# Sparse attention with a feed-forward block: sampled, end and neighbouring keys gathered into one buffer, and edge queries without their zero half

## The chip, the cores and the metric

The kernel runs on 1 core of one Trainium2 chip. The metric is the device time of one execution in microseconds (us). The kernel before takes 754.68 us as the median of 3 runs (754.65 to 762.38). The change is judged by the same metric on the same kind of chip.

## The reference

```python
batch, n_heads, seq, head_dim = (4, 8, 768, 64)     # q, k, v: float32
block, n_rand = 32, 3                               # 24 blocks of 32 positions
scores = scale * np.matmul(q, k.transpose(0, 1, 3, 2))
mask = np.abs(blk_i - blk_j) <= 1                   # neighbouring blocks
mask = mask | (blk_i == 0) | (blk_j == 0) | (blk_i == n_blocks - 1) | (blk_j == n_blocks - 1)
for qb in range(n_blocks):
    for kb in sampled_blocks[qb]:                   # 3 sampled blocks for each block of queries
        mask[qb * block:(qb + 1) * block, kb * block:(kb + 1) * block] = True
scores = np.where(mask, scores, -1000000000.0)
attn = np.exp(scores - np.max(scores, axis=-1, keepdims=True))
attn = attn / (np.sum(attn, axis=-1, keepdims=True) + 1e-09)
x = np.matmul(attn, v)                              # then (tokens, 512)
h = x @ w_in                                        # 512 -> 2048
g = h * erf(np.maximum(h, 0.0) + np.log1p(np.exp(-np.abs(h))))
return g @ w_out                                    # 2048 -> 512
```

A query of one of the 22 middle blocks sees 8 blocks of keys: the first and the last block of the sequence, three neighbours (its own and one on each side) and three sampled ones. A query of the first or the last block (an edge query) sees all 24.

## The kernel before, in words

The attention of one batch is cut into **units**. A middle unit `("m", b, u)` is two neighbouring middle blocks of queries in all 8 heads; there are 11 in a batch and 44 in all. An edge unit `("f", b, pr)` is the first and the last block of queries for one pair of heads; there are 4 in a batch and 16 in all. The feed-forward work is cut into groups of 256 tokens by 256 hidden values (`ff_first`, `ff_logs` and what follows); there are 96.

`scores` (lines 624 to 648) makes a unit's scores on TensorE in float32. `kx` holds one batch's keys in SBUF: two heads of 64 values one above the other on the 128 partitions (`a` is 0 or 1, the upper or the lower head of a pair), 24 blocks, 4 pairs of heads, 32 positions. For a middle unit it issues 32 small products, each of 64 rows by 32 queries. The 16 of `part` 0 take 96 columns (the three neighbours) from `kx`. The 16 of `part` 1 take 160 columns from `kbufs`: the first block, three sampled ones and the last one. There is one buffer for each block of queries, 4 in all. The scores of head half `a` lie in columns 512 `a` to 512 `a` + 511 of a PSUM tile of 128 partitions by 1024 columns; pair `pr` writes partitions 32 `pr` to 32 `pr` + 31.

For an edge unit `order_q` has copied the queries into `qm`, which is zero elsewhere, so that one product over all 128 rows gives both heads of a pair: the queries of `a` = 0 stand in the upper half of the rows, those of `a` = 1 in the lower half, and the zeros keep the heads apart. That is two products of 128 by 128, with 512 and 256 columns.

`gather` (lines 331 to 354) fills the key buffers on GpSimd (POOL): six copies of one sampled block (128 columns) a unit, and the two end blocks (256 columns) once a buffer and batch. `gather_v` (lines 359 to 386) brings the same blocks of values by DMA: neighbours and ends by SP, the sampled rows by an indirect DMA of POOL. Their order within a buffer has to be that of the score columns.

The first six units and the preparation of the weights come first, in an order that a scheduler chooses. From then on (`held`) each engine has its instructions in the order in which the loop over groups (lines 987 to 1042) emits them. One round of the loop issues on TensorE: the products with the values of an earlier unit (`po`), `ff_first` of one group (`h`, 24 products), the scores of one unit, `ff_second` of an earlier group (`o`, 12 products). Some rounds have no unit. `gathers` runs before `scores` in a round, so the keys of the next unit are asked for one round ahead; POOL's copies then wait until the unit that last read the buffer has its scores.

All instructions that these helpers record carry line 48 in the profile, so groups are told apart by the names of their tiles: `s_m` and `s_f` are the scores of middle and edge units, `kbuf` and `kx` the keys, `h` and `o` the feed-forward products.

Of the kernel before, what the change touches and what calls it, by code (L numbers as in the profile page):

```python
# [9 lines left out]
F32 = mybir.dt.float32  # L10
I32 = mybir.dt.int32
# [7 lines left out]
P = 128  # L19
BLOCK = 32  # L20
# [11 lines left out]
def sparse_attention_moe(ctx: ExitStack, tc: tile.TileContext, qT, kT, v, sampled, w_in, w_out, out):  # L32
# [26 lines left out]
    B, H, D, S = qT.shape  # L59
    NB = S // BLOCK  # L60
# [5 lines left out]
    NR = sampled.shape[1]  # L66
    KT = S // P
    HP = H // 2
# [74 lines left out]


    qts = {}
    qm = cp.tile([P, HP, 2, 2, BLOCK], F32, tag="qm", name="qm")
    dve.memset(qm, 0.0)

    def load_q(b, t):
        if b == 0 and 0 < t < 4:  # L150
# [12 lines left out]
    def queries(b, u):  # L163
        t, half = divmod(u, 2)
        return qts[b, t][:, :, half * 2 * BLOCK : (half + 1) * 2 * BLOCK].rearrange("p r (j c) -> p r j c", c=BLOCK)

    def order_q(b):
        qt = queries(b, NU)
        for a in range(2):
            dve.tensor_copy(qm[a * D : (a + 1) * D, :, :, a, :], qt[a * D : (a + 1) * D])  # L170

    QW = 4 * VW
    vraws = {}
# [20 lines left out]
    def pow2_bound(bound, tag, by_sum):  # L194

        top = st.tile([P, 1], F32, tag="top", name=f"top_{tag}")
        dve.reduce_max(top, bound, AX.X)
        if by_sum:  # L200
            allm = ps_h.tile([P, W], F32, tag="h", name=f"allm_{tag}")
            if tag[0] == "v":
                pe.matmul(allm[0:1, 1 : 1 + P], top, eye, start=True, stop=True)
                top = st.tile([P, 1], F32, tag="top", name=f"most_{tag}")[0:1]
                dve.reduce_max(top, allm[0:1, 1 : 1 + P], AX.X)
            allm = allm[:, :1]
            pe.matmul(allm, ones[: top.shape[0]], top, start=True, stop=True)
        else:
            allm = st.tile([P, 1], F32, tag="allm", name=f"allm_{tag}")
            pool.partition_all_reduce(allm, top, P, bass.bass_isa.ReduceOp.max)  # L210
        return allm

    def pow2_scale(allm, tag, squared):
        m = st.tile([P, 1], F32, tag="m", name=f"m_{tag}")
        dve.tensor_scalar_max(m, allm, 1e-37 if squared else 1e-19)
        e = st.tile([P, 1], I32, tag="e", name=f"e_{tag}")
        dve.tensor_scalar(e, m.bitcast(I32), 24 if squared else 23, None, ALU.logical_shift_right)
        zero = 63 if squared else 127
        s = st.tile([P, 1], F32, tag="s_" + tag[:2], name=f"s_{tag}", bufs=2)
        inv = st.tile([P, 1], F32, tag="i_" + tag[:2], name=f"i_{tag}", bufs=2)  # L220
        unit = float(1 << 23)
        dve.tensor_scalar(s.bitcast(I32), e, -unit, (127 + 13 + zero) * unit, ALU.mult, ALU.add)
        dve.tensor_scalar(inv.bitcast(I32), e, unit, (127 - 13 - zero) * unit, ALU.mult, ALU.add)
        return s, inv
# [101 lines left out]
    rows_of = []  # L326
    vgs = {}
    kgs, last_of = {}, {}
    kbufs = [cp.tile([P, NR + 2, HP, BLOCK], F32, tag=f"kg{n}", name=f"kbuf{n}") for n in range(KGS)]

    def gather(b, u):

        first, last = 1 + 2 * u, 3 + 2 * u
        (load,), blocks = nc.values_load_multi_w_load_instructions(
            samp[0:1, first * NR : last * NR],
            [mybir.EngineType.Pool],
            min_val=0,
            max_val=NB - 1,
            skip_runtime_bounds_check_because="sampled blocks are numbers of the sequence's blocks",
        )  # L340
        tc.keep_in_program_order(load)
        for i in range(first, last):
            n = (b * NM + i - 1) % KGS
            kg = kbufs[n]
            if last_of.get(n) != b:
                last_of[n] = b
                pool.tensor_copy(kg[:, 0 : NR + 2 : NR + 1], kxs[b][:, 0 : NB : NB - 1])
            for r in range(NR):
                n = blocks[(i - first) * NR + r]
                pool.tensor_copy(  # L350
                    kg[:, 1 + r].rearrange("p a c -> p (a c)"),
                    kxs[b].rearrange("p n a c -> p n (a c)")[:, bass.ds(n, 1), :].rearrange("p n c -> p (n c)"),
                )
            kgs[b, i] = kg

    ends_of = {}
    turn_of = [0]
# [1 line left out]
    def gather_v(b, i):  # L359

        n = turn_of[0] % VGS
        turn_of[0] += 1
        vg = vbufs[n]
        tab = vtab[b]
        if i < 0:
            rows = tab[: NB * BLOCK].rearrange("(k p) c -> p k c", p=P)
            sp.dma_start(vg, rows[:, -2 * i - 2 : -2 * i])
            ends_of.pop(n, None)
        else:
            low, high = max(i - 1, 1), min(i + 2, NB - 1)  # L370
            c = (low - i + 1) * BLOCK
            sp.dma_start(vg[c : c + (high - low) * BLOCK, 0], tab[low * BLOCK : high * BLOCK])
            if high - low < 3:
                c = 0 if i == 1 else 2 * BLOCK
                sp.dma_start(vg[c : c + BLOCK, 0], tab[NB * BLOCK :])
            if ends_of.get(n) != b:
                ends_of[n] = b
                ends = tab[: NB * BLOCK].rearrange("(n r) c -> r n c", r=BLOCK)[:, 0 : NB : NB - 1]
                sp.dma_start(vg[NR * BLOCK :], ends)
            pool.indirect_dma_start(  # L380
                out=vg[: NR * BLOCK, 1],
                out_offset=None,
                in_=tab,
                in_offset=bass.IndirectOffsetOnAxis(ap=rows_of[0][: NR * BLOCK, i - 1 : i], axis=0),
            )
        vgs[b, i] = vg
# [237 lines left out]
    def scores(unit):  # L624
        kind, b, n = unit
        s = ps_s.tile([P, 1024], F32, tag="s", name=f"s_{kind}_{b}_{n}")
        kx = kxs[b]
        if kind == "m":
            qt = queries(b, n)
            s5 = s.rearrange("p (a j c) -> p a j c", a=2, j=2)  # L630
            for part in range(2):
                for j in range(2):
                    i = 1 + 2 * n + j
                    for pr in range(HP):
                        for a in range(2):
                            o, d = slice(pr * BLOCK, (pr + 1) * BLOCK), slice(a * D, (a + 1) * D)
                            if part == 0:
                                place, keys = s5[o, a, j, : 3 * BLOCK], kx[d, i - 1 : i + 2, pr, :]
                            else:
                                place, keys = s5[o, a, j, 3 * BLOCK :], kgs[b, i][d, :, pr, :]  # L640
                            pe.matmul(place, qt[d, pr, j], keys, start=True, stop=True)
            softs[unit] = (s, HP, 256)
        else:
            q_ = qm[:, n].rearrange("p n a c -> p (n a c)")
            for c, e in ((0, 512), (512, S)):
                keys = kx[:, c // BLOCK : e // BLOCK, n, :]
                pe.matmul(s[:, c:e], q_, keys, start=True, stop=True)
            softs[unit] = (s[:, :S], 1, S)

    xTs = {}  # L650
# [3 lines left out]
    def values(b, u, part):  # L654
        po = ps_po.tile([P, 512], F32, tag="po", name=f"po_{b}_{u}_{part}")
        groups = range(4) if part is None else range(2 * part, 2 * part + 2)
        for gr in groups:
# [7 lines left out]
            for x, part_of, off in terms:  # L665
                for k in range(2 if u < NU else KT):
                    for a in range(2):
                        pr = 2 * p2_ + a
                        c = (2 * pr + r) * VW
                        w = slice(c + part_of.start, c + part_of.stop)  # L670
                        for j in range(2):
                            if u < NU:
                                pT = pts["m", b, u][:, (2 * r + j) * 4 + x * 2 + k]
                                vg = vgs[b, 1 + 2 * u + j][:, k, w]
                                col = pr * BLOCK
                            else:
                                pT = pts["f", b, pr][:, x * KT + k]
                                vg = vgs[b, -1 - k // 2][:, k % 2, w]
                                col = j * 64 + r * BLOCK
                            todo.append((2 * a + j, pT[:, col : col + BLOCK], vg, at_gr + off))  # L680
            for m, (o, lhs, rhs, c) in enumerate(todo):
                pe.matmul(
# [8 lines left out]
    def norm(b, u, part):  # L691
# [1 line left out]
        tag = f"{b}_{u}_{part}"  # L693
        gr = slice(0, 4) if part is None else slice(2 * part, 2 * part + 2)
        n = gr.stop - gr.start
        rinv = st.tile([P, 4], F32, tag="rinv", name=f"rinv_{tag}")[:, :n]
        first = 0 if part is None else 1
        dve.tensor_scalar(rinv, po[:, first * PO + D : (first + n - 1) * PO + D + 1 : PO], EPS * 2.0**P_SHIFT, None, ALU.add)
        dve.reciprocal(rinv, rinv)
# [145 lines left out]
    def next_queries(m):  # L845

        b, n = divmod(m, per)
        if n == NU - 1:
            order_q(b)
# [231 lines left out]
```

## Time and profile before

| what | value |
|---|---|
| median of 3 runs | 754.68 us (754.65 to 762.38) |
| the profiled execution's own time | 764.91 us |
| its span | 763.1 us |
| granted TensorE clock, mean | 0.975 |
| TensorE (PE) busy | 686.3 us, 90% |
| ScalarE (ACT) busy | 591.9 us, 78% |
| VectorE (DVE) busy | 575.4 us, 75% |
| GpSimd (POOL) busy | 201.6 us, 26% |

The durations further down come from the one profiled execution, whose span begins with its first instruction and ends with its last. PE counts matmuls; PEld counts weight loads, which overlap them. A float32 product has two matmul records and two weight loads in the trace (16 products of a unit are 32 records), and records of small products that run side by side overlap, so that a group's busy time is less than its count times its mean.

### The profile page before, as it was taken

How to read it: one execution, taken by the hardware profiler on the slowest of the kernel's cores; microseconds unless marked ns; L12 is line 12 of the kernel's file. 1: busy time of each engine (PE TensorE's matmuls, PEld its weight loads, DVE VectorE, ACT ScalarE, POOL GpSimd, SP SyncE). 2: the span in 40 equal slices, each digit the busy share in tenths (PEclk: the TensorE clock that was granted, in tenths of full speed). 3: DMA queues.
4: the chain of work that ended last, by engine and by line, in shares of the span. 5: the costliest groups of instructions: out<-in, count | busy, mean ns of one | idle time of the engine just before them, and what ended most of it. 6: DMA issues, size and time to landing. Idle time of an engine off the chain costs nothing.

```text
span 763.1 us, 24883 instructions
## 1 busy us (share of the span) xinstructions
PE 686.3 (90%) x10400; PEld 450.6 (59%) x10400; DVE 575.4 (75%) x1122; ACT 591.9 (78%) x1023; POOL 201.6 (26%) x413
## 2 busy tenths in 40 slices
PE   1336887998999999999999999999999999999997
PEld 0213554655655666666566666666666666667663
DVE  6983999978777788778687878787777786665453
ACT  2544999878877887878888887888788887776774
POOL 3026624303364313130533312033433120000000
PEclk9976998998999999999999999999999999999999
DMA  8999835896599999855997799938988677130000
GB/s 304 415 293 283 257 91 119 195 224 154 136 224 211 193 208 182 212 144 87 250 191 162 187 166 194 251 89 185 223 157 182 130 147 168 29 77 2 8 29 27
DMA packets 188048, 129.36 MB, mean 170 GB/s; under 512 B 137760, under 2 KB 160928, under 8 KB 186912
## 3 DMA queue, kind: packets, MB, share of 16 engines
q1 hardware_dynamic: 173584, 84.50, 54.1%
q10 hardware_dynamic: 8464, 25.43, 10.4%
q0 software_dynamic: 5888, 17.84, 9.6%
q8 instruction: 81, 1.33, 0.7%
q14 instruction: 31, 0.25, 0.1%
HBM read 82.81 MB, written 12.95 MB: 125 GB/s over the span
## 4 chain that ended last, share of the span: by engine, by line
PE 78%; DMA 6%; DVE 5%; ACT 5%; issue 3%; SPq 2%; ACTq 0%; DVEq 0%
PE h L48 31%; PE o L48 31%; PE s_m L48 7%; PE po_None L48 4%; PE s_f L48 3%; SPq L48 2%; DMA vbuf<-vtab 2%; DMA wo<-in_w_in_dram 2%; DMA vtab<-vn 1%; ACT x L48 1%; PE po L48 1%; DVE room L48 1%; DMA vbuf<-in_v_dram 1%; ACT pf_m L48 1%; DVE less_m L48 1%
## 5 line engine op out<-in xcount | busy, mean ns | idle before, releaser
L48 PE MATMUL h<-xT,wi 128*128 128x256 f16 x2304 | 272.3, 275 | 5.0 <-DVE y L48 4.5
L48 PE MATMUL o<-wo,g 128*128 128x512 f16 x1152 | 264.5, 379 | 0.5 <-DVE g L48 0.2
L48 PEld LDWEIGHTS <-wi 128*128 128x128 f16 x2304 | 223.7, 99 | 45.8 <-DVE y L48 4.6
L48 ACT ACTIVATE x<-x 128x512 f32<-128x512 f32 x288 | 181.6, 631 | 8.9
L48 PEld LDWEIGHTS <-g 128*128 128x128 f16 x1152 | 109.5, 98 | 127.4 <-issue 6.6
L48 POOL DMA_INDIRECT vbuf<-vtab,idx x88 | 96.5, 1097 | 185.1 <-PE po_None L48 130.3
L48 DVE SCALAR_TENSOR_TENSOR y<-y,x 128x512 f32<-128x512 f32 x96 | 67.1, 699 | 95.0 <-ACT x L48 91.6
L48 POOL COPY kbuf<-kx 128x128 f32 (+1 forms) x280 | 87.3, 357 | 94.4 <-PE s_m L48 79.8
L48 ACT ACTIVATE x<-h,isg 128x512 f32<-128x512 f32 x96 | 65.4, 682 | 49.2 <-PE h L48 31.9
L48 ACT ACTIVATE y<-y 128x512 f32<-128x512 f32 x96 | 59.7, 622 | 32.9 <-DVE y L48 32.9
L48 ACT ACTIVATE pf_m<-s_m,less_m 128x256 f32<-128x256 f32 x176 | 68.9, 473 | 19.7 <-DVE less_m L48 18.7
L48 DVE SCALAR_TENSOR_TENSOR g<-y,sums,g 128x512 f16<-128x512 f32 x96 | 73.1, 762 | 3.4
L48 DVE SCALAR_TENSOR_TENSOR y<-y,h 128x512 f32<-128x512 f32 x96 | 65.2, 679 | 0.1
L48 ACT ACTIVATE y<-x 128x512 f32<-128x512 f32 x96 | 60.4, 631 | 3.0
L48 DVE TENSOR_REDUCE less_m<-s_m 128x4 f32<-128x1024 f32 x44 | 53.6, 1218 | 11.7 <-PE s_m L48 11.6
L48 PEld LDWEIGHTS <-pT_m 128*32 128x32 f16 x3168 | 35.4, 98 | 33.9 <-issue 31.4
L48 PE MATMUL po_None<-vbuf,pT_m 128*32 128x65 f16 (+2 forms) x3168 | 41.9, 205 | 13.2 <-issue 12.5
L48 PE MATMUL s_m<-kbuf,qt 64*32 64x160 f32 x1408 | 48.2, 316 | 3.7 <-issue 2.8
L48 DVE TENSOR_SCALAR g<-y,sums 128x512 f16<-128x512 f32 x96 | 48.0, 500 | 3.4
L48 PE MATMUL s_m<-kx,qt 64*32 64x96 f32 x1408 | 31.6, 259 | 20.4 <-ACT kx L48 13.3
L48 DVE SCALAR_TENSOR_TENSOR p_m<-pf_m,p_m 128x1024 f16<-128x1024 f32 x38 | 46.4, 1221 | 0.3 <-issue 0.3
L48 DVE TENSOR_TENSOR x<-xf,x 128x256 f16<-128x256 f32 x44 | 18.8, 426 | 31.7 <-ACT x L48 31.6
(110 smaller groups left out, 609.8 us busy)
## 6 DMA issues: line engine op xcount, KB each, us to landing
vbuf<-vtab SPq DMA_DIRECT2D x80, 195.0 KB
vraw<-in_v_dram ACTq DMA_DIRECT2D x9, 768.0 KB
vtab<-vn SPq DMA_DIRECT2D x16, 390.0 KB
vbuf<-vtab SPq DMA_DIRECT2D x12, 520.0 KB
wo<-in_w_out_dram ACTq DMA_DIRECT2D x6, 1024.0 KB
qt<-in_qT_dram SPq DMA_DIRECT2D x20, 256.0 KB
kr<-in_kT_dram ACTq DMA_DIRECT2D x12, 384.0 KB
vbuf<-vtab SPq DMA_DIRECT2D x32, 130.0 KB
```

The source lines that it names most:

```text
L48: done = call(*args, **kwargs)
```

## The change

`gather` now fills one buffer of 14 blocks for a unit instead of two of 5. Its slots are: first, three sampled, last (of the first block of queries); four neighbouring blocks `first - 1` to `last`; first, three sampled, last (of the second block of queries). The four neighbours are one new POOL copy of 512 columns. The first block of queries reads slots 0 to 7, the second slots 6 to 13, both 8 blocks, so `scores` issues 16 products of 256 columns where it issued 32, and reads `kx` no more. For the second block of queries the neighbours now come ahead of ends and samples, so `gather_v` places its values in that order. An edge unit issues four products of 64 rows by 64 queries (two heads, two pieces of columns) straight from the loaded queries; `qm` and `order_q` are gone. Several small statistics tiles have fewer buffers.

```diff
@@ load and order queries
-    qm = cp.tile([P, HP, 2, 2, BLOCK], F32, tag="qm", name="qm")
-    dve.memset(qm, 0.0)
...
-    def order_q(b):
-        qt = queries(b, NU)
-        for a in range(2):
-            dve.tensor_copy(qm[a * D : (a + 1) * D, :, :, a, :], qt[a * D : (a + 1) * D])
...
-        top = st.tile([P, 1], F32, tag="top", name=f"top_{tag}")
+        top = st.tile([P, 1], F32, tag="top", name=f"top_{tag}", bufs=1)
...
-    kbufs = [cp.tile([P, NR + 2, HP, BLOCK], F32, tag=f"kg{n}", name=f"kbuf{n}") for n in range(KGS)]
+    kbufs = [cp.tile([P, 14, HP, BLOCK], F32, tag=f"kg{n}", name=f"kbuf{n}") for n in range(KGS // 2)]
...
-        for i in range(first, last):
-            n = (b * NM + i - 1) % KGS
-            kg = kbufs[n]
-            if last_of.get(n) != b:
-                last_of[n] = b
-                pool.tensor_copy(kg[:, 0 : NR + 2 : NR + 1], kxs[b][:, 0 : NB : NB - 1])
+        n = (b * NU + u) % (KGS // 2)
+        kg = kbufs[n]
+        if last_of.get(n) != b:
+            last_of[n] = b
+            for j in range(2):
+                pool.tensor_copy(kg[:, 9 * j : 9 * j + 5 : 4], kxs[b][:, 0 : NB : NB - 1])
+        pool.tensor_copy(kg[:, 5:9], kxs[b][:, first - 1 : last + 1])
+        for j in range(2):
             for r in range(NR):
-                n = blocks[(i - first) * NR + r]
+                n = blocks[j * NR + r]
                 pool.tensor_copy(
-                    kg[:, 1 + r].rearrange("p a c -> p (a c)"),
+                    kg[:, 9 * j + 1 + r].rearrange("p a c -> p (a c)"),
                     kxs[b].rearrange("p n a c -> p n (a c)")[:, bass.ds(n, 1), :].rearrange("p n c -> p (n c)"),
                 )
-            kgs[b, i] = kg
+        kgs[b, u] = kg
...
-            for part in range(2):
-                for j in range(2):
-                    i = 1 + 2 * n + j
-                    for pr in range(HP):
-                        for a in range(2):
-                            o, d = slice(pr * BLOCK, (pr + 1) * BLOCK), slice(a * D, (a + 1) * D)
-                            if part == 0:
-                                place, keys = s5[o, a, j, : 3 * BLOCK], kx[d, i - 1 : i + 2, pr, :]
-                            else:
-                                place, keys = s5[o, a, j, 3 * BLOCK :], kgs[b, i][d, :, pr, :]
-                            pe.matmul(place, qt[d, pr, j], keys, start=True, stop=True)
+            for j in range(2):
+                for pr in range(HP):
+                    for a in range(2):
+                        o, d = slice(pr * BLOCK, (pr + 1) * BLOCK), slice(a * D, (a + 1) * D)
+                        keys = kgs[b, n][d, 6 * j : 6 * j + 8, pr, :]
+                        pe.matmul(s5[o, a, j], qt[d, pr, j], keys, start=True, stop=True)
             softs[unit] = (s, HP, 256)
         else:
-            q_ = qm[:, n].rearrange("p n a c -> p (n a c)")
+            qt = queries(b, NU).rearrange("p r j c -> p r (j c)")
             for c, e in ((0, 512), (512, S)):
-                keys = kx[:, c // BLOCK : e // BLOCK, n, :]
-                pe.matmul(s[:, c:e], q_, keys, start=True, stop=True)
+                for a in range(2):
+                    d = slice(a * D, (a + 1) * D)
+                    keys = kx[d, c // BLOCK : e // BLOCK, n, :]
+                    pe.matmul(s[d, c:e], qt[d, n], keys, start=True, stop=True)
```

The order of the instructions shows it at three places. On TensorE, unit 5 of batch 2, between the feed-forward products `h` and `o` (in brackets stand the engines whose semaphores an instruction waits for). Before:

```order
L48 MATMUL h_1_2_1_7331<-xT_1_2_5590,wi_123 128x256
L48 MATMUL s_m_2_5_7386<-kx_2_5383,qt_2_2_6797 32x96 [waits DVE_49,Activation_49]
L48 MATMUL s_m_2_5_7386<-kx_2_5383,qt_2_2_6797 32x96 x15
L48 MATMUL s_m_2_5_7386<-kbuf2_121,qt_2_2_6797 32x160 [waits Pool_49]
L48 MATMUL s_m_2_5_7386<-kbuf2_121,qt_2_2_6797 32x160 x7
L48 MATMUL s_m_2_5_7386<-kbuf3_122,qt_2_2_6797 32x160 [waits Pool_49]
L48 MATMUL s_m_2_5_7386<-kbuf3_122,qt_2_2_6797 32x160 x7
L48 LDWEIGHTS g_1_1_6_7230
L48 MATMUL o_1_2_6404<-wo_124,g_1_1_6_7230 128x512
```

The same unit in the changed kernel:

```order
L48 MATMUL h_1_2_1_6935<-xT_1_2_5262,wi_119 128x256
L48 MATMUL s_m_2_5_6991<-kbuf1_118,qt_2_2_6431 32x256 [waits DVE_49,Activation_49,Pool_49]
L48 MATMUL s_m_2_5_6991<-kbuf1_118,qt_2_2_6431 32x256 x7
L48 MATMUL s_m_2_5_6991<-kbuf1_118,qt_2_2_6431 32x256 [waits Pool_49]
L48 MATMUL s_m_2_5_6991<-kbuf1_118,qt_2_2_6431 32x256 x7
L48 LDWEIGHTS g_1_1_6_6834
L48 MATMUL o_1_2_6068<-wo_120,g_1_1_6_6834 128x512
```

Three places at which TensorE waits have become two, and the first of them now waits for POOL as well.

On TensorE, the first edge unit of batch 2 in the changed kernel; before, there stood one product of 128 by 512 and one of 128 by 256 from `qm`:

```order
L48 MATMUL s_f_2_0_8342<-kx_2_5053,qt_2_5_7733 64x512 [waits DMAHW5_49,PE_49,Activation_49]
L48 MATMUL s_f_2_0_8342<-kx_2_5053,qt_2_5_7733 64x512
L48 MATMUL s_f_2_0_8342<-kx_2_5053,qt_2_5_7733 64x256 x2
L48 LDWEIGHTS g_2_0_0_8215 [waits DVE_49]
L48 MATMUL o_2_0_8347<-wo_120,g_2_0_0_8215 128x512 [waits Activation_49]
```

Two products have become four, which alternate between the upper and the lower head.

On POOL, the copies of one middle unit in the changed kernel (`ISA` rows set the address of a sampled block); before, there were the same six copies of 128x128, into two buffers:

```order
L327 TENSOR_LOAD samp_103
L48 COPY kbuf1_118<-kx_1_2151 128x512
L48 ISA
L48 COPY kbuf1_118<-kx_1_2151 128x128
L48 ISA
L48 COPY kbuf1_118<-kx_1_2151 128x128
...
L48 DMA vbuf3_107<-vtab_1_112,idx_242 96x1040
L48 DMA vbuf4_108<-vtab_1_112,idx_242 96x1040
```

One copy of 512 columns comes ahead of the six, and the two indirect DMAs of the values stand behind all seven.

## Rows read from the trace of the kernel before

**Rows 1.** The page, its first line and section 1.
```profile
span 763.1 us, 24883 instructions
...
PE 686.3 (90%) x10400; PEld 450.6 (59%) x10400; DVE 575.4 (75%) x1122; ACT 591.9 (78%) x1023; POOL 201.6 (26%) x413
```

**Rows 2.** The page, section 4: the chain of waits, shares by engine.
```profile
PE 78%; DMA 6%; DVE 5%; ACT 5%; issue 3%; SPq 2%; ACTq 0%; DVEq 0%
```

**Rows 3.** Busy time by stretch: bounds, length, engines (instructions), TensorE clock, DMA share, GB/s.
```profile
100.00:128.00 28.00, 22.07 (x262) 16.02 (x261) 27.57 (x69) 27.61 (x53) 7.58 (x10) 0.89 0.36 91
...
400.00:500.00 100.00, 99.51 (x1584) 66.21 (x1586) 80.30 (x154) 84.20 (x146) 24.75 (x48) 1.00 0.98 191
```

**Rows 4.** Groups of PE by shape: count | busy us, mean ns | idle before, releasers.
```profile
L48 PE MATMUL s_f<-kx,qm 128*128 128x512 f32 x32 | 16.5, 597 | 0.1
...
L48 PE MATMUL s_f<-kx,qm 128*128 128x256 f32 x32 | 9.5, 379 | 0.0
```

**Rows 5.** Timeline of PE, one middle unit: start, length, operation, count.
```profile
361.53 0.56 PE L48 MATMUL s_m<-kx,qt 64*32 64x96 f32 x32
361.88 0.86 PE L48 MATMUL s_m<-kbuf,qt 64*32 64x160 f32 x32
362.67 2.76 PE L48 MATMUL o<-wo,g 128*128 128x512 f16 x12
```

**Rows 6.** Busy time of instructions on s_m by stretch; PE is the first number.
```profile
240.00:296.00 56.00, 7.45 (x320) 4.90 (x320) 6.08 (x5) 8.09 (x21) 1.00 0.98 194
...
380.00:456.00 76.00, 9.58 (x448) 6.62 (x448) 8.51 (x7) 12.27 (x32) 1.00 0.94 178
...
128.00:640.00 512.00, 55.19 (x2304) 35.31 (x2304) 43.85 (x36) 56.08 (x144) 0.99 0.88 181
```

**Rows 7.** Timeline of PE, a middle unit with pauses inside it.
```profile
297.37 0.56 PE L48 MATMUL s_m<-kx,qt 64*32 64x96 f32 x32
297.73 0.65 PE L48 MATMUL s_m<-kbuf,qt 64*32 64x160 f32 x15
298.89 0.47 PE L48 MATMUL s_m<-kbuf,qt 64*32 64x160 f32 x3 [0.52 <-issue]
299.63 0.56 PE L48 MATMUL s_m<-kbuf,qt 64*32 64x160 f32 x14 [0.27 <-issue]
300.13 2.76 PE L48 MATMUL o<-wo,g 128*128 128x512 f16 x12
```

**Rows 8.** Timeline of PE, one edge unit.
```profile
472.30 1.46 PE L48 MATMUL s_f<-kx,qm 128*128 128x512 f32 x4
473.59 1.67 PE L48 MATMUL o<-wo,g 128*128 128x512 f16 x7
```

**Rows 9.** The chain of waits in order of time: start, length, what.
```profile
358.87 2.73 PE h L48 x24
361.60 1.14 PE s_m L48 x62
362.74 2.69 PE o L48 x12
...
463.71 2.62 PE h L48 x24
466.33 2.59 PE o L48 x12
```

**Rows 10.** Groups of POOL by shape.
```profile
L48 POOL COPY kbuf<-kx 128x128 f32 x264 | 80.2, 346 | 80.4 <-PE s_m L48 79.8 <-POOL kbuf L48 0.2
L48 POOL COPY kx<-kr 128x768 f32<-128x768 f32 x12 | 10.3, 856 | 52.0 <-DMA kr<-in_kT_dram 52.0
L48 POOL COPY kbuf<-kx 128x256 f32<-128x256 f32 x16 | 8.5, 533 | 14.0 <-ACT kx L48 11.9 <-POOL kx L48 2.0
```

**Rows 11.** Timeline of POOL between two middle units.
```profile
362.60 1.48 POOL L48 COPY kbuf<-kx 128x128 f32 x6 [7.82 <-PE s_m L48]
```

**Rows 12.** Groups of DVE by shape: the copies into qm.
```profile
L48 DVE COPY qm<-qt 64x256 f32<-64x256 f32 x8 | 2.8, 352 | 0.1
```

More of the change, by code (lines that the diff above doesn't have):

```diff
@@ L203, in pow2_bound @@
                 pe.matmul(allm[0:1, 1 : 1 + P], top, eye, start=True, stop=True)
-                top = st.tile([P, 1], F32, tag="top", name=f"most_{tag}")[0:1]
+                top = st.tile([P, 1], F32, tag="top", name=f"most_{tag}", bufs=1)[0:1]
                 dve.reduce_max(top, allm[0:1, 1 : 1 + P], AX.X)
@@ L208, in pow2_bound @@
         else:
-            allm = st.tile([P, 1], F32, tag="allm", name=f"allm_{tag}")
+            allm = st.tile([P, 1], F32, tag="allm", name=f"allm_{tag}", bufs=1)
             pool.partition_all_reduce(allm, top, P, bass.bass_isa.ReduceOp.max)
@@ L213, in pow2_scale @@
     def pow2_scale(allm, tag, squared):
-        m = st.tile([P, 1], F32, tag="m", name=f"m_{tag}")
+        m = st.tile([P, 1], F32, tag="m", name=f"m_{tag}", bufs=1)
         dve.tensor_scalar_max(m, allm, 1e-37 if squared else 1e-19)
-        e = st.tile([P, 1], I32, tag="e", name=f"e_{tag}")
+        e = st.tile([P, 1], I32, tag="e", name=f"e_{tag}", bufs=1)
         dve.tensor_scalar(e, m.bitcast(I32), 24 if squared else 23, None, ALU.logical_shift_right)
         zero = 63 if squared else 127
-        s = st.tile([P, 1], F32, tag="s_" + tag[:2], name=f"s_{tag}", bufs=2)
-        inv = st.tile([P, 1], F32, tag="i_" + tag[:2], name=f"i_{tag}", bufs=2)
+        s = st.tile([P, 1], F32, tag="s_" + tag[:2], name=f"s_{tag}", bufs=1)
+        inv = st.tile([P, 1], F32, tag="i_" + tag[:2], name=f"i_{tag}", bufs=1)
         unit = float(1 << 23)
@@ L370, in gather_v @@
             low, high = max(i - 1, 1), min(i + 2, NB - 1)
-            c = (low - i + 1) * BLOCK
-            sp.dma_start(vg[c : c + (high - low) * BLOCK, 0], tab[low * BLOCK : high * BLOCK])
+            odd = i % 2
+            near, end = odd * BLOCK, 0 if odd else NR * BLOCK
+            c = near + (low - i + 1) * BLOCK
+            sp.dma_start(vg[c : c + (high - low) * BLOCK, odd], tab[low * BLOCK : high * BLOCK])
             if high - low < 3:
-                c = 0 if i == 1 else 2 * BLOCK
-                sp.dma_start(vg[c : c + BLOCK, 0], tab[NB * BLOCK :])
+                c = near + (0 if i == 1 else 2 * BLOCK)
+                sp.dma_start(vg[c : c + BLOCK, odd], tab[NB * BLOCK :])
             if ends_of.get(n) != b:
@@ L378, in gather_v @@
                 ends = tab[: NB * BLOCK].rearrange("(n r) c -> r n c", r=BLOCK)[:, 0 : NB : NB - 1]
-                sp.dma_start(vg[NR * BLOCK :], ends)
+                sp.dma_start(vg[end : end + BLOCK], ends)
             pool.indirect_dma_start(
-                out=vg[: NR * BLOCK, 1],
+                out=vg[near : near + NR * BLOCK, 1 - odd],
                 out_offset=None,
@@ L678, in values @@
                                 vg = vgs[b, -1 - k // 2][:, k % 2, w]
-                                col = j * 64 + r * BLOCK
+                                col = r * 64 + j * BLOCK
                             todo.append((2 * a + j, pT[:, col : col + BLOCK], vg, at_gr + off))
@@ L695, in norm @@
         n = gr.stop - gr.start
-        rinv = st.tile([P, 4], F32, tag="rinv", name=f"rinv_{tag}")[:, :n]
+        rinv = st.tile([P, 4], F32, tag="rinv", name=f"rinv_{tag}", bufs=2)[:, :n]
         first = 0 if part is None else 1
@@ L847, in next_queries @@
         b, n = divmod(m, per)
-        if n == NU - 1:
-            order_q(b)
         if n < NU - 1 and n % 2 == 0 and (b or n >= 6):
```

## The prediction

> **What bounds the kernel now.** I read the first section of the page, then the chain of waits, then the busy time by stretch. TensorE is busy 90% of the span and no other engine over 78% [rows 1]; 78% of the chain that ended last is TensorE's [rows 2]. In the stretch from 400 to 500 us TensorE is busy 99.5 of 100 us at full clock, while ScalarE has 84 and VectorE 80 [rows 3]. So from about 128 us on, once the preparation is over, a microsecond taken off TensorE comes off the end, and one added there is paid in full. Before that VectorE and ScalarE are busy 27.6 of 28 us [rows 3], so TensorE's scores are cheap there. The timeline of TensorE shows the place of the change: a middle unit's scores stand between `h` and `o` with no pause on either side [rows 5].
>
> **Middle units, before.** A float32 record takes 597 ns with 512 columns and 379 with 256 [rows 4]; the difference, 218 ns for 256 columns, is 0.85 ns a column. An edge unit agrees: four records, twice 512 and twice 256 columns, 1536 x 0.85 = 1.31 us, and from its first start to the next product it takes 473.59 - 472.30 = 1.29 [rows 8]. In a middle unit 32 records of 96 columns pass in 361.88 - 361.53 = 0.35 us [rows 5]. One of them needs 82 ns, so 32 x 82 / 350 = 7.5 are under way at once: all eight places that products of 64 rows by 32 queries have in the array. Per unit the streaming is then 4 x (96 + 160) x 0.85 = 0.87 us. This unit takes 1.14 us in the chain [rows 9], so 0.27 us are not streaming: 0.02 in the first part (0.35 - 4 x 0.082) and the rest in the second (0.79 - 4 x 0.136 = 0.25). It is among the shortest. Five units between 240 and 296 us and seven between 380 and 456 us (64 records each) are busy 7.45 + 9.58 = 17.03 us, 1.42 each [rows 6]; the last records overlap the next product by 0.56 + 0.86 - 0.21 - 1.14 = 0.07 us (the two parts, less their own overlap, against the 1.14) [rows 5], so they hold TensorE for 1.35.
>
> **Middle units, after.** The columns are the same, so the 0.87 us stay. What goes is half of the records and one of three waits, that between the neighbours' and the other keys' products (the order of the instructions shows them). The cost of one piece of 256 columns has no row. Its lower bound is 0.89 us, streaming with the overhead of the first part alone; the upper one is the present 1.35, if the irregular time comes from what stands around the scores and not from their split. I take 1.08, a little under the 1.14 of the shortest unit, as that unit still has the second part's start. The gain is 0.27 us a unit. Between 128 and 640 us there are 36 units (2304 records) [rows 6]: 9.7 us. The other 8 lie in the preparation, where I count nothing.
>
> **Edge units.** Two products of 128 rows become four of 64 rows by 64 queries, for the upper and lower head, on opposite quarters of the array. If the two heads run side by side, the streaming stays at 1.29 us [rows 8]. New is that the array changes from one shape of product to another on the way in and out. The nearest rows: `o` takes 2.69 us in the chain behind a middle unit's scores and 2.59 behind `h`, and `h` 2.73 where another shape stands ahead of it and 2.62 behind `o` [rows 9], 0.1 us a change. Twice that for 16 units is 3.2 us more. Bounds: nothing, and the full second pass told of below.
>
> **POOL.** 44 copies of 512 columns are added. The nearest rows are 533 ns for 256 columns and 856 for 768 [rows 10]; between them lies about 0.7, and the slope from 128 to 256 columns (346 to 533) would give 0.91. At 0.9 that is 40 us on an engine with 201.6 busy [rows 1]. It lies beside TensorE's work: the six copies wait 79.8 us for `s_m` [rows 10], that is, they start as soon as the scores that last read the buffer are done, and one set takes 1.48 us from 362.60 [rows 11], and the scores that need it come two rounds later, each of at least 2.62 + 1.14 + 2.59 = 6.35 us [rows 9]: over 12 us on. The products' first wait is now for POOL too, and all of `o` stands behind it on TensorE; with 10 us of room left it is met early. The indirect DMAs behind the copies start up to 0.9 us later; their values are used three rounds on. If that cover were gone, 36 x 0.9 = 32 us would stand on the path.
>
> **The rest.** VectorE loses 8 copies of 352 ns [rows 12] and a memset, which lie beside TensorE's work: nothing. The queries' tile is now read until the last edge unit and refilled one unit later, so SP's load finds it free: nothing. Fewer buffers of the statistics: nothing, as writer and reader follow each other anyway. In the preparation the scheduler has put VectorE's and ScalarE's work in another order, and the first scores need one more copy (0.9 us) before VectorE wants them: no estimate better than nothing, with 3 us either way.
>
> **Sum.** -9.7 + 3.2 = -6.5 us. The profiled execution took 764.9 us (its span is 763.1), so 758.4 of its kind; it is 10.2 us over the median. Against the median of 754.7 the same difference gives **748.2 us**. Bounds of the terms: -16.6 (0.89 a unit, no price for the edge units) to +3.2, each 3 us wider for the preparation: 735 to 761.
>
> **Rivals.**
> *One head waits for the other in edge units* (slower). In middle units the two heads write different halves of the score tile, columns 0 to 511 and 512 to 1023. In edge units both write the same columns, on different partitions, from different rows of the array. No row of before has two such products at once. If they take turns, an edge unit streams 1.29 us more: 16 x 1.29 = 20.6, and 748.2 + 20.6 = 768.8. It decides from 6.5 / 16 = 0.4 us a unit on. Against it: the four pairs of heads of a middle unit also write the same columns on different partitions and do run at once, though from the same rows. [...]
>
> *Records start in strict order* (no change). Each product is two records on the same place of the array. If the second held up the next product, an edge unit's records of 0.43, 0.43, 0.43, 0.43, 0.22, 0.22, 0.22, 0.22 us would overlap only in neighbours of different heads: 1.72 us and not 1.29, 16 x 0.43 = 6.9 more, 755.1. Against it: at most two could then be under way, and the middle unit shows 7.5 [rows 5]. [...]
>
> *The irregular time stays* (no change). If units still hold TensorE for 1.35 us, only the edge units' price is left: 754.7 + 3.2 = 757.9. For it: I know the 0.2 us over the shortest unit only as a mean. Against it: the shortest and the longer units have the same columns, and what differs between them lies inside.
>
> *Pauses go too* (faster). Some units hold TensorE far longer: one from 297.37 to 300.13, 2.76 us, with pauses in which it waits for nothing the profile shows [rows 7]. All 36 are busy 55.19 us [rows 6], 4.1 over 36 x 1.42, and the pauses themselves come on top. If they come from the number of instructions, and are there in undisturbed executions as well, halving them gives back 4 to 8 us more: 742. Against it: the profiled execution is 10 us over the median, so these pauses may belong to it alone.
>
> **How the numbers follow.** My forecast has 0.42, heads taking turns 0.2, strict order 0.08, irregular time staying 0.14, pauses going 0.14, with 0.02 for a preparation that goes worse. The likeliest case alone spans 742 to 753 by the preparation and the unit's 1.08 (0.98 to 1.14). No more than 2 in 10 may be left out, so both outer cases are needed: 740 to 769. A measurement of this kernel can tell about 1% from no change, 747.1 and 762.2. Faster: all of the pauses and some 45% of my case, 0.33. Slower: heads taking turns and the worse preparation, 0.22. Within 1%: 0.45.
>
> **What would show it.** In the profile after, middle units: 32 records of 256 columns and a start-to-start time of 1.0 to 1.15 us, with little spread. Edge units: 8 records from the first start to `o` in 1.3 to 1.5 us; 2.6 would be turns, 1.7 strict order. `h` and `o` around edge units 0.1 longer. POOL busy about 240 us, the 512-column copies near 0.9, and no TensorE wait for `kbuf` beyond the first units. The prediction is wrong if TensorE shows idle time ahead of `s_m` for POOL, or if the time before 128 us moves by more than 3 us.

## The result: 0.65% slower, and the profile after

The changed kernel takes 764.35 us, the median of 22 runs (757.26 to 779.58). The kernel before, run beside it, takes 758.44 us (22 runs, 753.29 to 763.73). The ratio is 1.0065, with a 95% interval of 1.0038 to 1.0092: about 5 us slower, where 6.5 us faster was forecast. Ratios and their intervals, here and below, leave out runs over 1.5% above the fastest of their kernel (one of the 22 of after), so that the ratio gives 4.9 us where the medians differ by 5.9. The profiled execution of after took 767.07 us.

The page after, first line, section 1 and the chain's shares, which answer to [rows 1, 2]:

```profile
span 765.3 us, 22183 instructions
...
PE 678.3 (89%) x9056; PEld 426.3 (56%) x9056; DVE 578.5 (76%) x1113; ACT 592.2 (77%) x1023; POOL 229.7 (30%) x457
...
PE 56%; DVE 15%; DMA 13%; ACT 11%; issue 3%; SPq 1%; ACTq 0%
```

TensorE has 8 us less to do and the span is 2 us longer. Its share of the chain fell from 78% to 56%: more of the chain that ended last is now VectorE's, DMA's and ScalarE's. That share does not rank kernels: it is 72% in a second profile of before, 62% in one of the change, and 53% in the fastest kernel of the experiments below.

Timeline of TensorE after, one edge unit and two middle units (answers to [rows 5, 8]):

```profile
355.24 1.51 PE L48 MATMUL s_f<-kx,qt 64*64 64x512 f32 x8
356.68 2.76 PE L48 MATMUL o<-wo,g 128*128 128x512 f16 x12
...
368.47 1.09 PE L48 MATMUL s_m<-kbuf,qt 64*32 64x256 f32 x32
369.49 2.76 PE L48 MATMUL o<-wo,g 128*128 128x512 f16 x12
372.10 2.78 PE L48 MATMUL h<-xT,wi 128*128 128x256 f16 x24
374.81 1.09 PE L48 MATMUL s_m<-kbuf,qt 64*32 64x256 f32 x32
375.83 2.76 PE L48 MATMUL o<-wo,g 128*128 128x512 f16 x12
```

From its first start to the next product a middle unit takes 1.02 us (369.49 - 368.47), an edge unit 1.44 (356.68 - 355.24). The work of the change itself does on TensorE nearly what was forecast. The same for the groups by shape (answers to [rows 4, 10]):

```profile
L48 POOL COPY kbuf<-kx 128x128 f32 x264 | 82.9, 361 | 0.0
...
L48 PE MATMUL s_m<-kbuf,qt 64*32 64x256 f32 x1408 | 53.7, 403 | 16.5 <-POOL kbuf L48 15.3 <-issue 1.1
...
L48 POOL COPY kbuf<-kx 128x512 f32<-128x512 f32 x44 | 28.8, 654 | 82.9 <-PE s_m L48 82.9
...
L48 PE MATMUL s_f<-kx,qt 64*64 64x512 f32 x64 | 17.2, 615 | 0.2 <-ACT pf_m L48 0.2
...
L48 PE MATMUL s_f<-kx,qt 64*64 64x256 f32 x64 | 9.6, 376 | 0.0
```

The 15.3 us for `kbuf` are the first unit's, ahead of everything else; no unit of the steady part waits for POOL.

**Where the time went: the preparation.** The first feed-forward product starts when the last of four pieces of the first `xT` is written by VectorE. Timeline of TensorE, that product before:

```profile
104.12 3.44 PE L48 MATMUL h<-xT,wi 128*128 128x256 f16 x30 [0.55 <-DVE xT L48]
...
123.28 5.30 PE L48 MATMUL h<-xT,wi 128*128 128x256 f16 x24 [4.50 <-DVE y L48]
135.21 2.79 PE L48 MATMUL h<-xT,wi 128*128 128x256 f16 x24
```

and after:

```profile
111.87 2.78 PE L48 MATMUL h<-xT,wi 128*128 128x256 f16 x24 [0.52 <-DVE xT L48]
...
128.73 2.79 PE L48 MATMUL h<-xT,wi 128*128 128x256 f16 x24 [3.57 <-DVE y L48]
139.31 0.94 PE L48 MATMUL h<-xT,wi 128*128 128x256 f16 x7
```

The first product is 7.8 us later, the fourth group 5.5, the fifth 4.1. (The last row is cut off by the end of the window at 140 us; the group has 24 products.) Second profiles of both kernels put the fifth group at 133.9 and 139.4 us, 5.5 apart. In the pair shown, the fourth group of before takes 5.30 us at a granted clock of 0.50, after 4.50 us of waiting, and that of after 2.79 at 1.00, after 3.57 us of waiting, which narrows the gap for a while. The busy time from the start to that piece of `xT`, before (third pair of numbers: VectorE):

```profile
0.00:103.65 103.65, 50.76 (x922) 28.78 (x923) 82.26 (x177) 57.81 (x111) 42.01 (x92) 0.88 0.93 294
```

and after:

```profile
0.00:111.41 111.41, 52.05 (x701) 26.50 (x702) 89.92 (x185) 61.81 (x120) 52.94 (x101) 0.86 0.90 281
```

VectorE is idle for 21.4 us in the one (103.65 - 82.26) and 21.5 in the other. What differs is its work: 7.7 us more of it stand ahead of that piece. None of that work is new, since the change gives VectorE nine instructions fewer (1113 against 1122). In the traces 5.2 of the 7.7 us are steps that decode pieces of `w_out` (they read the tile `raw`) and 1.7 a reduction over the values; both were moved ahead. The scheduler, which gives the preparation its order, chose another one. In it VectorE comes to the decoding of `w_out` earlier and waits for its load; its timeline after:

```profile
70.20 1.17 DVE L48 TENSOR_SCALAR room<-wo 128x1024 int32<-128x1024 int32 x1 [1.85 <-DMA wo<-in_w_out_dram]
...
73.89 0.39 DVE L48 SCALAR_TENSOR_TENSOR xT<-turned,xT 128x256 f16<-128x256 f32 x1
78.75 0.87 DVE L48 TENSOR_SCALAR room<-wo 128x1024 int32<-128x1024 int32 x1 [4.46 <-DMA wo<-in_w_out_dram]
```

Before, VectorE's one long wait there was for TensorE, 11.19 us until 67.80, and from then on it worked almost without a gap: 34.77 of the 35.85 us until 103.65.

### The profile page after: what moved, and what is told of

It is laid out like the page before. It is cut to its first block, busy times and chain, and to the rows that moved or that the text cites. A ratio compares the mean times of both kernels' runs of the same rounds, so it can differ in the third digit from the quotient of the medians.

```text
span 765.3 us, 22183 instructions
## 1 busy us (share of the span) xinstructions
PE 678.3 (89%) x9056; PEld 426.3 (56%) x9056; DVE 578.5 (76%) x1113; ACT 592.2 (77%) x1023; POOL 229.7 (30%) x457
## 4 chain that ended last, share of the span: by engine, by line
PE 56%; DVE 15%; DMA 13%; ACT 11%; issue 3%; SPq 1%; ACTq 0%
PE h L48 23%; PE o L48 23%; ACT x L48 4%; DMA pT_m<-p_m 3%; PE s_f L48 3%; PE s_m L48 3%; PE po_None L48 3%; DVE y L48 2%; DMA vraw<-in_v_dram 2%; DMA wo<-in_w_out_dram 2%; ACT pf_m L48 2%; DVE room L48 2%; DVE less_m L48 2%; DVE xf L48 2%; DMA vbuf<-vtab 2%
## 5 line engine op out<-in xcount | busy, mean ns | idle before, releaser
L48 POOL COPY kbuf<-kx 128x128 f32 (+2 forms) x324 | 116.6, 409 | 96.8 <-PE s_m L48 82.9
L48 POOL DMA_INDIRECT vbuf<-vtab,idx x88 | 94.2, 1071 | 157.4 <-PE po_None L48 108.5
L48 PE MATMUL s_m<-kbuf,qt 64*32 64x256 f32 x1408 | 53.7, 403 | 16.5 <-POOL kbuf L48 15.3
L48 ACT ACTIVATE p_m<-pf_m 128x1024 f16<-128x1024 f32 x38 | 40.2, 1058 | 5.9 <-DMA pT_m<-p_m 4.8
L48 PEld LDWEIGHTS s_m<-kbuf,qt 64*32 64x32 f32 x1408 | 22.4, 110 | 33.7 <-POOL kbuf L48 15.5
```

The costliest lines, as they stand in the source:

```text
L48: done = call(*args, **kwargs)
```

## Experiments

The letters of the theories hold within each expectation. Ratios are to the kernel before, run beside them on the same chip; intervals are of 95%. What a trace shows comes from one profiled execution of each kernel.

**The change with the old preparation.** The first six units are scored from `kx` and the key buffers in two parts and have no added copy; everything else is the change.

```diff
-        pool.tensor_copy(kg[:, 5:9], kxs[b][:, first - 1 : last + 1])
+        if b or u >= FIRST:
+            pool.tensor_copy(kg[:, 5:9], kxs[b][:, first - 1 : last + 1])
...
+            if b or n >= FIRST:
...
+            else:
+                for part in range(2):
...
+                                if part == 0:
+                                    place, keys = s5[o, a, j, near : near + 3 * BLOCK], kx[d, i - 1 : i + 2, pr, :]
+                                else:
+                                    place, keys = s5[o, a, j, rest : rest + 5 * BLOCK], kgs[b, n][d, 9 * j : 9 * j + 5, pr, :]
```

> The changed kernel, except that the six units of the preparation are scored as before, in two passes from kx and from the key buffers, without the copy of the neighbours; the other 38 middle units and all edge units are as in the change. Theory A (the loss sits in the preparation, whose instructions the scheduler puts in another order when the first scores change; the rest gains what was forecast): the first feed-forward product starts near 104 us as before and not near 112, and the time is 5 to 8 us under that of before, ratio 0.990 to 0.994. Theory B (the loss sits in the later part: TensorE's gain turns into waits for the DMA transposes and for ScalarE): the time stays above that of before, ratio 1.002 to 1.008.

Measured: ratio 0.9991 (0.9944 to 1.0039), 12 runs; the first `h` at 104.4 us, middle units as in the change. Against the change in the same session (1.006) that is 5.2 us back, with room from 0.5 to 10 by the intervals of the two ratios; the medians of all 12 runs of each are 2.2 us apart (759.14 and 761.32). Its fifth group starts at 136.8 us, between before (135.2 and 133.9) and the change (139.3 and 139.4): the old preparation comes back in part. So the preparation carries the loss, but how large its share is these runs tell only roughly. With it undone the kernel is not 6.5 us faster than before, only level with it: a second term was wrong too.

**The opposite:** the first six units as in the change, all later middle units in two parts without the added copy, edge units as in the change.

```diff
-        pool.tensor_copy(kg[:, 5:9], kxs[b][:, first - 1 : last + 1])
+        if b == 0 and u < FIRST:
+            pool.tensor_copy(kg[:, 5:9], kxs[b][:, first - 1 : last + 1])
```

> The opposite: the six units of the preparation are scored as in the change, with the neighbours' copy and one product of 256 columns; the other 38 middle units in two passes from kx and the key buffers, without that copy. Edge units as in the change. Theory A: the first feed-forward product near 112 us, middle units at about 1.35 us, time 10 to 15 us over before, ratio 1.013 to 1.020. Theory B: ratio 1.000 to 1.005.

Measured: 1.0129 (1.0045 to 1.0212), 6 runs; first `h` at 111.5 us, median of the middle units 1.14 us and not the 1.35 expected. The two costs without the gain: 9.8 us, where 3.8 for the edge units (next run) and 5.2 for the preparation make 9.0.

**The edge units alone,** put into the kernel before:

```diff
-            q_ = qm[:, n].rearrange("p n a c -> p (n a c)")
...
-                pe.matmul(s[:, c:e], q_, keys, start=True, stop=True)
+                for a in range(2):
+                    d = slice(a * D, (a + 1) * D)
+                    keys = kx[d, c // BLOCK : e // BLOCK, n, :]
+                    pe.matmul(s[d, c:e], qt[d, n], keys, start=True, stop=True)
```

> The kernel before with the edge units alone changed: no zero half, four products of 64 by 64. Theory A and B alike: edge units 1.44 us in place of 1.29, 16 times 0.15 = 2.4 us, ratio 1.002 to 1.005. A theory C, that the edge units carry the whole loss (ScalarE late behind them), expects 1.006 to 1.009.

Measured: 1.0024 (0.9977 to 1.0071), 12 runs. Edge units take 1.44 us (the median of 16, first start to the next product) where they took 1.29, and the `h` ahead of them 2.72 where it took 2.63. That is 16 x (0.15 + 0.09) = 3.8 us. The time of this run alone does not exclude theory C (1.006 to 1.009); the run with the old preparation does, as it has the new edge units too and its interval ends at 1.0039. The middle units of this kernel are those of before, and their median was 1.14 us, not the 1.37 of the execution that the prediction read.

**The change once more,** unedited, beside these three:

> The changed kernel unchanged, on the same chip as the three others. All theories: ratio 1.004 to 1.009, first feed-forward product near 112 us. If the first product comes near 104 us here, the preparation's length varies from run to run and theory A falls.

Measured: 1.006 (1.0019 to 1.0101), 12 runs; first `h` at 112.1 us, median of the middle units 1.03 us. The middle units and the first product are as in the first profile of after, and yet its span was 757.4 us, against 765.3, so one span says little.

**The kernel before once more.** Unedited, one profiled execution.

> The kernel before, profiled a second time. Theory A (the 1.37 us of a middle unit belong to the one execution that was profiled): median 1.14 us between 128 us and the end, and a span some us under 763. Theory B (they belong to the split into products of 96 and 160 columns with other work around): 1.3 us or more again. First feed-forward product near 104 us by both.

Measured: span 757.9 us, median of the middle units 1.14 us, first `h` at 102.9. Theory A holds for the usual unit. But some units still stood far longer. Timeline of TensorE in this execution, the end of one such unit (it starts at 284.76 us and takes 5.3 us, with the pause of 3.20 inside it) and the next:

```profile
288.49 0.40 PE L48 MATMUL s_m<-kx,qt 64*32 64x96 f32 x6 [3.20 <-issue]
...
290.05 3.40 PE L48 MATMUL o<-wo,g 128*128 128x512 f16 x12
...
298.47 0.56 PE L48 MATMUL s_m<-kx,qt 64*32 64x96 f32 x32
298.82 0.85 PE L48 MATMUL s_m<-kbuf,qt 64*32 64x160 f32 x32
299.61 0.60 PE L48 MATMUL o<-wo,g 128*128 128x512 f16 x2
```

The second takes 299.61 - 298.47 = 1.14 us, as its like did in [rows 5]. The busy time of the scores from 128 to 640 us (answers to [rows 6], where it was 55.19), before in this execution:

```profile
128.00:640.00 512.00, 46.52 (x2272) 32.31 (x2255) 43.88 (x36) 56.09 (x144) 0.99 0.87 181
```

after, first profile:

```profile
128.00:640.00 512.00, 40.00 (x1152) 17.68 (x1152) 43.79 (x36) 56.16 (x144) 0.98 0.85 181
```

and the change once more:

```profile
128.00:640.00 512.00, 39.44 (x1152) 17.77 (x1152) 43.75 (x36) 56.02 (x144) 0.99 0.87 182
```

So 15.2 us of gain by the first pair of profiles is 7.1 by the second pair (some half a microsecond too little, as 128 us cuts the first unit in two there, 2272 records for 2304). Most of the disagreement is in the kernel before.

**The gain without the two costs.** A buffer of 12 slots: three samples of the second block of queries, first, four neighbours, last, three samples of the first block. Each block of queries reads two runs of four slots, five apart, so the end blocks are shared and `qm` fits again. Edge units and the first six units are as before.

```diff
-    kbufs = [cp.tile([P, 14, HP, BLOCK], F32, tag=f"kg{n}", name=f"kbuf{n}") for n in range(KGS // 2)]
+    kbufs = [cp.tile([P, 12, HP, BLOCK], F32, tag=f"kg{n}", name=f"kbuf{n}") for n in range(KGS // 2)]
...
-                        keys = kgs[b, n][d, 6 * j : 6 * j + 8, pr, :]
+                                at_, cut = (0, 0) if j else (2, 1)
+                                keys = kg[:, at_ : at_ + 10].rearrange("p (g n) c -> p g n c", g=2)[:, :, cut : cut + 4]
```

> The change without its two costs: middle units after the sixth as in the change, one product of 256 columns (from a buffer of 12 slots in which the two blocks of queries share the end blocks, so that the products read two runs of four blocks), edge units with their queries beside zeros as before, and the first six units as before. Theory A (three terms that add up: middle units 36 x (1.14 - 1.03) = -4.1 us, edge units 16 x 0.15 = +2.4, preparation +6): only the first term is left, 4 us faster than before, ratio 0.994 to 0.996, middle units 1.03 us, edge units 1.29, first feed-forward product at 103 to 105 us. Theory B (middle units before take the 1.37 us of the first profile in most executions): 36 x 0.34 = 12 us faster, ratio 0.984. Theory C (what TensorE saves is lost again to waits for ScalarE): ratio 1.000, with more idle time of TensorE behind the units.

Measured: 0.9927 (0.9890 to 0.9963), median 753.39 us of 9 runs: 5.5 us faster than before (2.8 to 8.3). It beats both kernels. Page of this kernel:

```profile
span 750.0 us, 22458 instructions
...
PE 671.4 (90%) x9184; PEld 432.9 (58%) x9184; DVE 581.2 (77%) x1122; ACT 592.4 (79%) x1023; POOL 220.8 (29%) x447
```

Middle units take 1.03 us, edge units 1.29, the first `h` starts at 104.4 us. The gain of the middle units is between theory A's 4 us and theory B's 12, nearer to A. The preparation is not quite that of before: the fifth group starts at 136.5 us, 1.3 to 2.6 later than in the two profiles of before, so the middle units may be worth somewhat more than 5.5 us.

**Added work or another order?** Two mixes in the preparation: only the first of the six units new (one added copy), and only the last four new (four added copies, none ahead of the first scores). Each is one line against the change with the old preparation, here where the copy is issued, and alike where the scores are:

```diff
-        if b or u >= FIRST:
+        if b or u < 1 or u >= FIRST:
```

```diff
-        if b or u >= FIRST:
+        if b or u >= 2:
```

> The change, but of the first six units only the first is scored from a buffer that holds the neighbours; units 1 to 5 are scored from two places as before. So the preparation has one added copy of 512 columns instead of six. Theory A (the order in which the scheduler puts the preparation decides, and that order differs from the one before as much as the change's own): the first feed-forward product anywhere from 102 to 114 us, not in proportion to the added work. Theory B (the added copies and the wait for them decide): one sixth of the change's 7.7 us, so 105 to 106 us, or all of it, 112, if the copy ahead of the first scores is what costs.

> The opposite mix: of the first six units the first two are scored from two places as before and units 2 to 5 from a buffer that holds the neighbours, so four added copies of 512 columns. Theory A (the order decides): the first feed-forward product anywhere from 102 to 114 us; together with the run that has one added copy, the times do not rise with the number of added copies. Theory B (the added work decides): four sixths of 7.7 us, 109 us, or 104 if only the copy ahead of the first scores costs.

Measured, one execution of each: with one copy the first `h` starts at 117.6 us and the execution takes 782.76 us; with four copies at 111.7 and 765.29 us (before beside them: 757.87). Timeline of TensorE, one copy:

```profile
113.33 2.23 PE L48 MATMUL rest<-wi,room 128*128 128x512 f32 x3
...
116.42 1.12 PE L48 MATMUL rest<-wi,room 128*128 128x512 f32 x2
...
117.64 2.79 PE L48 MATMUL h<-xT,wi 128*128 128x256 f16 x24
...
150.99 2.79 PE L48 MATMUL h<-xT,wi 128*128 128x256 f16 x24
```

The change's six copies gave 111.9. The delay does not rise with the added work, and one sixth of it cost the most. That excludes theory B in the forms in which it stands. With one copy VectorE starts to write the fourth piece of `xT` at 112.5 us, 1.1 us later than in the change (111.4), behind 89.4 us of work (89.9 in the change). The rest of the delay is TensorE's own order: it has other products of the preparation (`rest`, `turned` and products with the values) ahead of `h` until 117.6. So the amount of VectorE work ahead of `xT` does not tell when the first `h` starts.

**The change's work in another order.** All six units new, but the program asks for four steps of the weights' preparation behind each of them instead of three.

```diff
-        later(3)
+        later(4)
```

> The change with all its work (six first units scored from the new buffer, six added copies of 512 columns), but the program asks for four steps of the weights' preparation behind each of the first six units where it asked for three. That alone makes the scheduler choose another order: the VectorE work that stands ahead of the fourth piece of the first xT is 84.4 us by the durations of before's instructions, against 89.1 in the change and 82.9 before. Theory A (the order decides, through the VectorE work ahead of the fourth xT): first feed-forward product at 105 to 107 us instead of 112, and 3 to 5 us faster than the change, ratio to before 0.999 to 1.003. Theory B (the added copies and the new scores in the preparation cost the time): 111 to 113 us again, ratio 1.006.

Measured: first `h` at 108.9 us, 3 us earlier than in the change, but the ratio is 1.0049 (1.0017 to 1.0080), 12 runs: no difference from the change (1.006) that can be told. Timeline of TensorE:

```profile
108.89 2.79 PE L48 MATMUL h<-xT,wi 128*128 128x256 f16 x24
...
126.43 2.45 PE L48 MATMUL h<-xT,wi 128*128 128x256 f16 x21
...
144.00 4.72 PE L48 MATMUL h<-xT,wi 128*128 128x256 f16 x24
```

The fifth group starts at 144.0 us where the change had 139.3. The expectation failed: the same work in another order moved the preparation by several us in both directions, as theory A says, but the VectorE work ahead of the fourth piece of `xT` tells when that piece is written (106.6 us here, with `h` behind other products of TensorE until 108.9), and not when the preparation ends. And a fifth group that starts 4.7 us later did not make the kernel measurably slower: how much of a delay in the preparation reaches the end was not measured to a microsecond.

**The 12 slots in another order:** the same edit with `later(2)`.

> The version with 12 slots, edge units and first six units as before, with two steps of the weights' preparation asked for behind each of the first six units instead of three; the VectorE work ahead of the fourth piece of the first xT is 81.4 us against 82.9. Theory A (the order decides): first feed-forward product at 101 to 104 us, ratio to before 0.990 to 0.993. Theory B (order is not what counts): 104.4 us and 0.9927 again.

Measured: first `h` at 103.9 us, ratio 0.9940 (0.9906 to 0.9975), 12 runs; fifth group at 137.6 us where the 12 slots had 136.5. No gain from the order, and the version's gain over before repeated in another session.

## Why the prediction was wrong

**The first step that failed: the preparation.** It said "no estimate better than nothing, with 3 us either way". It was worth some 5 us: the fifth group starts 4.1 us later in the first pair of profiles and 5.5 in the second, and the change against itself with the old preparation gives 5.2 (0.5 to 10). This alone would have left the change 1.3 us faster (-6.5 + 5.2); the sign turned only together with the second step. The prediction had seen that the order changes and that VectorE is busy 27.6 of 28 us there [rows 3], and yet gave a change of its order the price nothing. What was open to it: the new order lists how much VectorE work stands ahead of the fourth piece of `xT`. By the durations of before's instructions that is 82.9 us before and 89.1 after; the traces show 82.26 and 89.92. The prediction's own condition for being wrong, a move of over 3 us before 128 us, was met: the fourth group starts at 128.7 instead of 123.3. Why each order ends the preparation when it does stays open; the runs show that the order alone moves it by several us, and that the delay does not follow the amount of added work. The fewer buffers of the statistics are not its cause by themselves: the run with the old preparation has them, and its first `h` is at 104.4 us.

**The second step, mis-sized: the middle units.** The mechanism held: 16 products a unit, 1.03 us, and in the two profiles of the change little spread. Predicted were 0.27 us a unit and 9.7 us in all; measured by itself the gain is 5.5 us. The 1.35 us that it started from was a mean over the one execution at hand. In a second execution, and in every other kernel that scores in two parts, the usual unit took 1.14. By medians the gain is 36 x (1.14 - 1.03) = 4.0 us. The rest may be pauses inside units: the means over 36 units were 1.65 and 1.47 us in the two profiles of before and 1.05 and 1.03 in the two of after. But they do not go with the split alone: over all profiles the means are 1.25 to 1.65 us with two parts (four profiles) and 1.03 to 1.36 with one (eight), and the highest of these, the 12 slots in another order, has a unit of 5.5 us. The rival "pauses go too" was partly right, and part of it is given back at products whose probabilities are still being transposed by DMA: TensorE's waits there, from 140 us on, come to 0 and 1.6 us in the two profiles of before, 7.7 and 6.3 in the two of the change, and 4.8 in the 12 slots. So the premise that from 128 us on each microsecond taken off TensorE comes off the end held only in part. That TensorE simply comes earlier to these products fits the rows, but no run separates it. Timeline of TensorE after:

```profile
224.19 1.50 PE L48 MATMUL po_None<-vbuf,pT_m 128*32 128x65 f16 x72 [4.14 <-DMA pT_m<-p_m]
237.38 1.50 PE L48 MATMUL po_None<-vbuf,pT_m 128*32 128x65 f16 x72 [3.52 <-DMA pT_m<-p_m]
```

and in the second execution of before:

```profile
227.86 0.88 PE L48 MATMUL po_None<-vbuf,pT_m 128*32 128x65 f16 x72 [1.62 <-DMA pT_m<-p_m]
```

A second place is `o` behind an edge unit, which after waits for ScalarE to have stored the last output (4.8 and 2.5 us in all in the two profiles of the change, 0.2 and 1.3 in those of before):

```profile
474.65 1.51 PE L48 MATMUL s_f<-kx,qt 64*64 64x512 f32 x8
478.46 1.86 PE L48 MATMUL o<-wo,g 128*128 128x512 f16 x4 [2.30 <-ACT wi L48]
```

**What held.** Edge units: 1.44 us and 0.09 more for the `h` ahead of them, 3.8 us against the 3.2 forecast; the time of the edge units alone, 1.8 us, agrees within its interval. The strongest rival, heads taking turns, fell, and with it the strict order, at 1.44 us against 2.6 and 1.72. The 20.6 and 6.9 us that these two would have added were the author's estimates, and no run shows them; what the runs showed in their place is 0.15 us more an edge unit, 1.44 where it was 1.29. POOL: 229.7 us busy against 240 forecast, the added copy 654 ns against 0.9 us, and no wait for it in the steady part.

**The sum as measured:** -5.5 (middle units) + 3.8 (edge units) + 5.2 (preparation) = +3.5 us; the change measured 4.9, with 2.9 to 7.0 as its interval. The terms come from different runs, each with several us of room, so the agreement does not prove the split. That the measured 764.35 us lies within the stated 740 to 769 is luck: that part of the range stood there for heads that take turns, which did not happen.

## What to carry to other kernels

Where a scheduler chooses an order, an edit in one place re-deals the work of every engine that it schedules: compare the new order with the old one and add up, from the old trace's durations, what now stands ahead of the work that starts the next stage, before calling that stage unchanged. Here that sum told when one engine's piece was written, and neither the first product nor the end of the stage, so keep a stage that is already tuned as it is where you can, and apply the edit only behind it. A mean over one profiled execution can carry pauses that belong to it: start a term from the shortest units that repeat, and keep the rest as a rival.

## What the runs showed of the hardware

Two products from opposite halves of the array's rows, which write the same columns of PSUM on different partitions, overlap in time: in the changed kernel an edge unit of four such products passes in 1.44 us, close to the 1.29 of two products over all rows; taking turns would be twice 1.29. The eight records, four of 615 ns and four of 376 by their means, come to 3.96 us. In the unit at 355.24 us they start in four pairs, 7 ns apart within a pair; the four records of the unit of before at 472.30 start one by one, 0.43, 0.43 and 0.22 us apart. These runs show no turn-taking in time.

In the second execution of before, pauses of TensorE for nothing that the profile shows recur at one place of its instruction stream. With weight loads, products and the semaphore and drain instructions recorded between them counted from 0 in order of their start, eight steps of 0.66 to 3.45 us between successive starts stand at place 193 of a run of 256, 11.7 us in all after 140 us; the row at 288.49 above is one. In the first profiles the DMA queue `q8 instruction` moved 81 packets before and 71 after, of 16.4 KB each. Over four executions of kernels that score the steady middle units in two parts, the steps at that place of over 0.45 us come to 2.7 to 13.9 us; over eight that score in one, to 0 to 6.5. The two ranges overlap: whether the number of instructions bears on these pauses is not shown, and no run here separates their cause.
